# New due times and a new transfer model in the list scheduler of a spectral filter with a gated feed-forward

## The chip, the cores and the metric

The kernel runs on one core of one Trainium2 chip. The metric is the device time of one execution in microseconds (us). Before the change three timed runs gave 418.05, 418.27 and 419.44 us, the median is 418.27.

The engines are called as in the profile: PE (TensorE, matrix products), PEld (its weight load), DVE (VectorE), ACT (ScalarE), POOL (GpSimd) and SP (SyncE, which issues the DMA transfers). SPq is SP's queue.

## The reference

The input x has 2048 rows of 512 values. Cut to what matters:

```python
xn = _layernorm(x, axis=-1)
X = jnp.fft.rfft2(xn, axes=(-2, -1)) * (w_r + 1j * w_i)
s = jnp.fft.irfft2(X, s=(2048, 512), axes=(-2, -1))
gate = xn @ W_gate                      # 512 x 1376
up = xn @ W_up
h = gate * (gate > 0) * up
return x + s * silu(h @ W_down)         # 1376 x 512
```

So there are two branches from the same normalised rows: a global filter in the frequency domain over both axes, and a feed-forward with a rectified gate. Their product is added to x.

## The kernel before, in words

**Precision.** All matrix products run in f16, with each factor split into a high and a low half. Three passes (high by high, high by low, low by high) are summed in PSUM. The halves are made by ACT (high) and DVE (low), so each factor passes through both. Scales that are powers of two keep the halves in range; they are worked out on the chip from the weights themselves.

**The feed-forward** goes over four row blocks c = 0 to 3 of 512 rows and eleven tiles f of the 1376 hidden columns. `gu{c}_{f}_0` is the gate product and `gu{c}_{f}_1` the up product, each of 12 matmuls of 128x512; they have two accumulators in all. ACT makes `r`, DVE `h32 = r * up` and the low half in `h16`. `dn{c}_{i}` is the down product, for four quarters i of the output (dn0_23 holds quarters 2 and 3), with weights `wds` against `h16`. The weights come in seven groups g (`raw{g}`, loaded in f32; `wgu{g}` after the split; group 6 holds the tiles 9 and 10, `wgt` the last). For each group a small product `sum{g}` adds sums of squares over the partitions, and `p{g}` becomes its scale.

**The scale of the down weights** needs all groups: DVE reduces `md` to one column, the transfer `row_md` writes it to DRAM as a row (128 values), `rows_md` reads it back broadcast to all partitions, DVE takes `max_md` and makes `scd`. Only then can the eleven `wds` tiles be split, high half by ACT, low half by DVE, and the first dn follow (`greatest`, `down_scale` and `down_weights`, from L602, L620 and L642). The filter has the same pair of transfers, `row_mw` and `rows_mw`, after ACT has squared the eight loads `rw0` to `rw7` (`filter_scale`, L652).

**The filter** works on eight chunks. For each 256 rows, DVE folds the normalised rows (`eo`, `ee`, `xs`), they are split to `xs16`, `s1_{c}` is the first transform on PE, and its split result `t1_{c}` goes to DRAM (`A_d`, four transfers of 256 KB for two chunks). When all chunks are there, `at_{q}` reads A_d back for eight chunks q of frequencies, across all rows. Each goes through the PE products `y`, `xx`, `z` and `v`, with the filter `wt_{q}` on DVE and POOL between xx and z. The results go to DRAM (`C_d`), come back as `ct_{c}`, and `s2_{c}` is the last transform (`last_stage`); DVE unfolds it (`ye`, `sv`), multiplies by the gate and adds x (`xt`), and `out` is written.

**The transposed rows** that the feed-forward needs, `xT{c}`, come from x16 by a DMA transpose on SP's queue, one for each 256 rows (`turn`, from L406), except those of block 0, which PE turns.

**What sets the order.** Nothing is issued when it is written. Each operation is recorded as a step with an engine, an estimated cost, what it reads and writes, and perhaps a due time (`step`, L109). `run` (L128) then passes due times back along the dependencies, and builds a schedule by list: among the steps that can begin soon on an engine it takes the one with the earliest due time. It keeps a model of the free time of each engine, of one shared DMA path and of the buffers of each pool (`k4` with 12 buffers holds x16, xs and xs16 among others). The steps are issued in the order of the modelled start times, one in-order stream per engine, and an engine that meets a wait holds all that stands behind it. As all steps are issued there, nearly all instructions have line L73 in the profile.

The due times come from the tables at L33 to L50: `FIRSTS` for the first stage of the eight chunks, `MIDS` for the chunks of frequencies, `LASTS` for the last stage, `DOWN` and `FILTER` for the two scales, `STAGES`, `LOADS` and `LEADS` for normalising and loading.

Of the kernel before, what the change touches and what calls it, by code (L numbers as in the profile page):

```python
# [15 lines left out]
S, D, F = 2048, 512, 1376  # L16
# [13 lines left out]

T0, DOWN, FILTER, TICK = -0.157, 96.244, 153.189, 1.169  # L33
FIRSTS = [58.53, 65.2, 93.07, 106.1, 121.7, 135.1, 152.7, 170.3]
MIDS = [159.33, 168.39, 174.23, 204.59, 230.67, 248.77, 265.67, 291.5]
STAGES = [10.61, 2.71, 12.71, 21.79]
LASTS = [290.55, 307.89, 309.81, 329.49, 347.94, 358.12, 368.92, 380.6]
ENDS = [6.8, 11.54]
LOADS, LOADX = [4.73, 0, 8.57, None, None, None, None], [-30, -0.3]
FOLDS, FOLD_LEAD, MARGIN = ['DVE', 'DVE', 'DVE', 'DVE', 'DVE', 'DVE', 'DVE', 'DVE'], 33.902, 1.95  # L40
# [4 lines left out]
SQUARES, HALF = 32.321, 2  # L45
# [3 lines left out]
HALVES, HEADS, STATS = ('gu', 'F'), [None, 8.91], ((0, 1),)  # L49
LEADS = [None, 7.77, 8.01, 11.9, 7.52, 7.23, 8.44]  # L50


RANGES = ((0, 257, 0), (257, 512, 1))
# [26 lines left out]
class Plan:  # L80
# [25 lines left out]
        if name:  # L106
            self.tile(name, tag, None)

    def step(self, engine, cost, fn, reads=(), writes=(), due=None, lead=None, port=False, kb=0, margin=0., lag=None, mode=0):  # L109
# [3 lines left out]
        s.mode = mode  # L113
# [12 lines left out]
        return s  # L126

    def run(self):  # L128
        steps = self.steps
        for s in reversed(steps):  # L130
            s.due = 1e9 if s.due is None else s.due
            for d in s.deps:
                t = s.due - d.cost - d.lag
# [19 lines left out]
        for _ in steps:  # L153
            best = None
            for e, mine in todo.items():
                at = []
                for s in mine:
                    t = max([free[e]] + [d.end + (0. if d.engine == e == "PE" else d.lag + s.margin) for d in s.deps])
                    if s.lead is not None:
                        t = max(t, s.due - s.lead)  # L160
                    if s.port:
                        t = max(t, ports["POOL" if e == "DVE" else "DVE"])
# [6 lines left out]
                    for tag, k in need.items():  # L169
                        t = max(t, sorted(room[tag])[k - 1] + .15)  # L170
                    at.append((t, s))
                if at:
# [4 lines left out]
                    t, s = min(now, key=lambda k: (e == "PE" and k[1].mode != mode if mode else 0, k[1].due, k[1].order))  # L177
# [7 lines left out]
            t, s = best  # L185
# [9 lines left out]
            free[e] = t + s.cost  # L195
            s.end = free[e]
            if s.kb:
                dma = max(dma, s.end) + s.kb / 340
                s.end = dma
            if s.port:  # L200
                ports[e] = s.end
            for n in holds[s]:
# [40 lines left out]
def kernel(ctx: ExitStack, tc: tile.TileContext, x, wg, wu, wd, wl, ew, sp, c_r, c_d, c_m, c_x, c_s, out):  # L243
# [162 lines left out]
    def turn(c, lows):  # L406
# [12 lines left out]
        def run():  # L419
            xt = T[f"xT{c // 2}"][:, 2 * (c % 2):2 * (c % 2) + 2]  # L420
            SP.dma_start_transpose(xt.rearrange("p i k r -> p (i k) r"), x16().rearrange("p i h d -> p (i h d)"))
        step("SP", 3.4, run, reads=[(f"x16_{c}", i, h) for i in range(2) for h in range(2)], 
             writes=[(f"xT{c // 2}", j, h) for j in range(2 * (c % 2), 2 * (c % 2) + 2) for h in range(2)], kb=100)

    def keep_busy(n):

# [824 lines left out]
```

## Time and profile before

| | before |
|---|---|
| median of 3 runs | 418.27 us (418.05 to 419.44) |
| profiled execution | 418.02 us |
| its span | 416.2 us |
| mean granted TensorE clock | 0.992 of full speed |
| PE busy | 401.3 us, 96% of the span |
| DVE busy | 305.0 us, 73% |
| ACT busy | 190.4 us, 46% |
| DMA | 51.79 MB, 124 GB/s over the span |

The span reaches from the first to the last instruction of the profiled execution. A row of the timelines has the start and the length of a run of like instructions in us, engine, line, operation, output<-input by the program's names without buffer numbers, the count, and in brackets the idle time ahead of it and what ended that. A row on waits has the engine that waited, what it waited for, the sum in us, how often, and the longest. A row on windows has a stretch, its length, and for each engine busy time and instructions, then the granted clock. A row on transfers has the count, the size and the us from issue to landing.

### The profile page before, as it was taken

What the parts mean: (1) busy time and instruction counts of PE and PEld (TensorE: products, weight loads), DVE (VectorE), ACT (ScalarE), POOL (GpSimd) and SP (SyncE); (2) the same over time, 40 slices, a digit from 0 to 9 for tenths busy, and PEclk for the clock granted to TensorE, in tenths of its full rate; (3) what the DMA queues carried; (4) which work ended last, traced back from release to release, by engine and by line L of the source; (5) the groups of instructions that cost most, each with busy time, mean ns of one, the idle gap of its engine ahead of it and who ended that gap; (6) DMA issues with size and microseconds to landing.
All of it is one profiled execution on the core that took longest, in us unless ns stands there. A gap on an engine that the chain in (4) does not pass through costs nothing.

```text
span 416.2 us, 7641 instructions
## 1 busy us (share of the span) xinstructions
PE 401.3 (96%) x3004; PEld 213.0 (51%) x3004; DVE 305.0 (73%) x656; ACT 190.4 (46%) x368; POOL 47.8 (11%) x72
## 2 busy tenths in 40 slices
PE   8999999899999998949999999999999999999996
PEld 6954445344444444416555555555554445444545
DVE  4889993998899969413998538768684326978984
ACT  5989833653454657113236334344434227224311
POOL 0000000000000000000631003303130007105400
PEclk9999999999999999988999999999999999999999
DMA  7970002218242996891000860035222184683342
GB/s 259 407 264 0 0 2 107 59 44 203 77 126 56 295 332 112 111 253 63 1 2 0 267 228 2 2 92 168 73 52 51 52 194 110 202 250 105 103 153 101
DMA packets 36436, 51.79 MB, mean 124 GB/s; under 512 B 15856, under 2 KB 17744, under 8 KB 36400
## 3 DMA queue, kind: packets, MB, share of 16 engines
q1 hardware_dynamic: 36400, 51.31, 42.2%
q8 instruction: 23, 0.38, 0.4%
q14 instruction: 13, 0.11, 0.1%
HBM read 35.55 MB, written 12.60 MB: 116 GB/s over the span
## 4 chain that ended last, share of the span: by engine, by line
PE 75%; DVE 12%; DMA 8%; ACT 2%; SPq 2%; issue 1%; DVEq 0%
PE gu L73 40%; PE dn L73 21%; PE z L73 3%; PE xx L73 3%; DVE h L73 2%; PE s L73 2%; DMA row_md<-md 2%; DVE wgu L73 2%; PE y L73 2%; DMA xT<-x 2%; DVE wds L73 2%; PE small L73 2%; DVE xs L73 2%; SPq L73 2%; PE v L73 2%; DMA at<-A_d 1%
## 5 line engine op out<-in xcount | busy, mean ns | idle before, releaser
L73 PE MATMUL gu<-xT,wgu 128*128 128x512 f16 (+1 forms) x960 | 208.3, 374 | 2.7 <-DVE h L73 2.2
L73 PEld LDWEIGHTS <-wgu 128*128 128x128 f16 x960 | 92.9, 98 | 109.6 <-issue 5.9
L73 PE MATMUL dn<-wds,h 128*128 128x512 f16 (+2 forms) x528 | 117.2, 372 | 1.9 <-DVE wds L73 1.5
L73 PEld LDWEIGHTS <-h 128*128 128x128 f16 (+1 forms) x594 | 54.4, 98 | 59.8 <-issue 5.4
L73 DVE TENSOR_TENSOR h<-gu,r 128x512 f32<-128x512 f32 (+3 forms) x52 | 33.1, 636 | 29.5 <-PE gu L73 28.0
L73 ACT ACTIVATE r<-gu 128x512 f32<-128x512 f32 (+2 forms) x44 | 25.7, 584 | 47.2 <-PE gu L73 47.1
L73 POOL TENSOR_TENSOR po<-tt,tt 128x256 f32<-128x256 f32 x16 | 14.6, 915 | 281.9 <-DVE tt L73 235.4
L73 ACT ACTIVATE h<-h 128x512 f16<-128x512 f32 (+1 forms) x44 | 27.3, 624 | 40.8 <-DVE h L73 40.6
L73 DVE TENSOR_TENSOR h<-h,h 128x512 f16<-128x512 f32 (+1 forms) x44 | 30.1, 692 | 7.3 <-ACT h L73 7.1
L73 POOL TENSOR_TENSOR ae<-zz 128x128 f32<-128x128 f32 (+1 forms) x32 | 20.1, 661 | 62.8 <-ACT zz L73 62.7
L73 DVE SCALAR_TENSOR_TENSOR tt<-xsp,cw,wt 128x512 f32<-128x512 f32 x32 | 26.1, 878 | 0.0
L73 ACT ACTIVATE g<-dn,cdi 128x512 f32<-128x512 f32 (+1 forms) x16 | 10.6, 672 | 29.9 <-PE dn L73 29.9
L73 DVE TENSOR_TENSOR z<-z,z 128x1024 f16<-128x1024 f32 x8 | 9.7, 1221 | 10.6 <-ACT z L73 10.6
L73 PE MATMUL gu<-xT,wgt 128*64 128x256 f16 (+1 forms) x144 | 17.0, 309 | 0.0
L73 ACT ACTIVATE a<-y 128x1024 f16<-128x1024 f32 x8 | 8.1, 1022 | 17.6 <-PE y L73 17.5
L73 DVE TENSOR_TENSOR a<-y,a 128x1024 f16<-128x1024 f32 x8 | 9.8, 1221 | 7.4 <-ACT a L73 7.4
L73 DVE TENSOR_TENSOR sv<-sv,g 128x512 f32<-128x512 f32 (+2 forms) x18 | 11.3, 661 | 4.8 <-ACT g L73 4.6
L73 DVE SCALAR_TENSOR_TENSOR wgu<-raw,p,wgu 128x512 f16<-128x512 f32 x20 | 14.2, 746 | 0.6 <-ACT wgu L73 0.6
L73 ACT ACTIVATE xs<-xs 128x1024 f16<-128x1024 f32 x8 | 8.3, 1053 | 13.1 <-DVE xs L73 13.1
L73 ACT ACTIVATE t<-v 128x1024 f16<-128x1024 f32 x8 | 8.1, 1022 | 13.1 <-PE v L73 13.1
L73 DVE TENSOR_TENSOR t<-v,t 128x1024 f16<-128x1024 f32 x8 | 9.7, 1222 | 5.9 <-ACT t L73 5.9
L73 PE MATMUL y<-cm,at 64*128 64x64 f16 x384 | 8.3, 201 | 5.8 <-DMA at<-A_d 5.8
(151 smaller groups left out, 455.1 us busy)
## 6 DMA issues: line engine op xcount, KB each, us to landing
A_d<-t SPq DMA_DIRECT2D x16, 256.0 KB, 3.9
rw<-in_wl SPq DMA_DIRECT2D x8, 512.0 KB, 6.5
wt<-in_wl SPq DMA_DIRECT2D x8, 512.0 KB, 4.8
at<-A_d SPq DMA_DIRECT2D x8, 512.0 KB, 6.6
C_d<-t SPq DMA_DIRECT2D x16, 256.0 KB, 3.5
ct<-C_d SPq DMA_DIRECT2D x16, 256.0 KB, 5.1
xt<-in_x SPq DMA_DIRECT2D x16, 256.0 KB, 4.1
out<-xt SPq DMA_DIRECT2D x15, 256.0 KB, 2.0
```

Of the source, the lines that this page charges most:

```text
L73: return lambda *args, **kw: self.tc.keep_in_program_order(f(*args, **kw))
```

## The change

The scheduler's model gets three new numbers, and every table of due times gets new values. The model now says of a DMA transpose that it costs SP 2.0 us instead of 3.4, that it moves 1300 KB on the DMA path instead of 100 (`TURNKB`), and that it blocks SP until 2.0 us after the DMA path is free (`block`). Other transfers go at 320 instead of 340 KB per us from 40 us on (`RATE`), and land 0.6 us later (`SLACK`). No step is added or removed, and no step's instructions change.

```diff
-T0, DOWN, FILTER, TICK = -0.157, 96.244, 153.189, 1.169
-FIRSTS = [58.53, 65.2, 93.07, 106.1, 121.7, 135.1, 152.7, 170.3]
...
+T0, DOWN, FILTER, TICK = 1.2, 93.937, 134.179, 1.169
+FIRSTS = [53.32, 98.69, 53.46, 108.61, 118.2, 143.13, 197.12, 178.58]
...
+RATE, SLACK, TURNKB = 320, .6, 1300
...
             if s.kb:
-                dma = max(dma, s.end) + s.kb / 340
-                s.end = dma
+                if s.block:
+                    s.end = free[e] = max(s.end, dma + s.block)
+                dma = max(dma, s.end) + s.kb / (340 if t < 40 else RATE)
+                s.end = dma + (SLACK if t > 40 else 0.)
...
-        step("SP", 3.4, run, reads=[(f"x16_{c}", i, h) for i in range(2) for h in range(2)], 
-             writes=[(f"xT{c // 2}", j, h) for j in range(2 * (c % 2), 2 * (c % 2) + 2) for h in range(2)], kb=100)
+        step("SP", 2., run, reads=[(f"x16_{c}", i, h) for i in range(2) for h in range(2)], 
+             writes=[(f"xT{c // 2}", j, h) for j in range(2 * (c % 2), 2 * (c % 2) + 2) for h in range(2)], kb=TURNKB, block=2.)
```

What it moves is seen in the order of the instructions. The first place is SP's queue between the scale of the filter and the first read of A_d (at_0). Before:

```order
L73 DMA row_mw_111<-mw_92 128x1
L73 DMA cm1_1884<-in_c_m 128x512
L73 DMA wt_1_1914<-in_wl 128x1024
L73 DMA_TRANSPOSE xT3_1825<-x16_7_1761 128x16x128
L73 DMA A_d_69<-t1_6_1912 128x1x1024 x2
L73 DMA A_d_69<-t1_7_1923 128x1x1024 x2
L73 DMA rows_mw_112<-row_mw_111 128x128
L73 DMA cm2_1977<-in_c_m 128x512
L73 DMA wt_1_1914<-E_d_71 2x2x128
L73 DMA wt_2_2005<-in_wl 128x1024
L73 DMA at_0_2017<-A_d_69 128x2x1024
```

and now the same place of SP's queue, from row_mw to at_0:

```order
L74 DMA row_mw_111<-mw_92 128x1
L74 DMA wt_0_1707<-in_wl 128x1024
L74 DMA cm1_1774<-in_c_m 128x512
L74 DMA E_d_71<-edge2_115 64x2x16 x2
L74 DMA rows_mw_112<-row_mw_111 128x128
L74 DMA A_d_69<-t1_5_1776 128x1x1024 x2
L74 DMA wt_0_1707<-E_d_71 2x2x128
L74 DMA A_d_69<-t1_6_1865 128x1x1024 x2
L74 DMA A_d_69<-t1_7_1876 128x1x1024 x2
L74 DMA wt_1_1928<-in_wl 128x1024
L74 DMA_TRANSPOSE xT3_1932<-x16_6_1631 128x16x128
L74 DMA at_0_1973<-A_d_69 128x2x1024
```

The writes of t1_6 and t1_7 have moved from behind the transposes of x16_6 (which stood just ahead of the first piece) and x16_7 to ahead of both; rows_mw has moved ahead of the writes, and the transpose of x16_7 behind at_0.

The second place is PE around sum6, the last of the sums that the scale of the down weights needs; its weights are named in the LDWEIGHTS rows. Before:

```order
L73 LDWEIGHTS wgu4_81
L73 MATMUL gu0_6_1_661<-xT0_267,wgu4_81 128x512
L73 MATMUL sum6_689<-m6_548,ones_94 128x4
L73 LDWEIGHTS wgu5_82
L73 MATMUL gu0_7_1_691<-xT0_267,wgu5_82 128x512
```

and now, on the same engine:

```order
L74 LDWEIGHTS wgu5_82
L74 MATMUL gu0_7_1_725<-xT0_237,wgu5_82 128x512
L74 MATMUL sum6_750<-m6_609,ones_94 128x4
L74 LDWEIGHTS wgu5_82
L74 MATMUL gu0_8_0_753<-xT0_237,wgu5_82 128x512
```

sum6 has moved from ahead of the products gu0_7_0 and gu0_7_1 to behind both. The third place is DVE right behind scd, where the low halves of the down weights (wds) are made. Before:

```order
L73 TENSOR_SCALAR scd_91<-rho_86,pd_107 128x11
L73 SCALAR_TENSOR_TENSOR wds_85<-wds_85,scd_91 128x512
L73 TENSOR_TENSOR h32_0_9_839<-gu0_9_1_801,r0_9_817 128x512
L73 SCALAR_TENSOR_TENSOR wds_85<-wds_85,scd_91 128x512
L73 TENSOR_TENSOR h16_0_9_842<-h32_0_9_839,h16_0_9_842 128x512
```

and now, on DVE from scd on:

```order
L74 TENSOR_SCALAR scd_91<-rho_86,pd_107 128x11
L74 TENSOR_TENSOR t1_0_899<-s1_0_847,t1_0_899 128x2x448
L74 SCALAR_TENSOR_TENSOR wds_85<-wds_85,scd_91 128x512
L74 TENSOR_TENSOR t1_0_899<-s1_0_847,t1_0_899 128x2x64
L74 TENSOR_TENSOR t1_2_917<-s1_2_874,t1_2_917 128x2x448
L74 SCALAR_TENSOR_TENSOR wds_85<-wds_85,scd_91 128x512
```

The large piece of t1_0 has moved ahead of the first low half of wds, and those of t1_2 between the first and the second. Besides, dn0_23 of tile 0 now follows dn0_0 and dn0_1 of tile 0 on PE, where before dn0_0 and dn0_1 of ten tiles came first; s1_6 and s1_7 stand ahead of gu1_8_1; the s2 steps of chunks 4, 6, 7 and 5 stand earlier in the last row block; and on SP the loads of x2 and x3 stand ahead of the last weight group, the first rw loads ahead of those of x6 and x7.

More of the change, by code (lines that the diff above doesn't have):

```diff
@@ L28 @@
 TAIL_COLS = ((0, 0, 96, 0, 256), (1, 64, 96, 96, 352), (1, 0, 64, 128, 192))
-T0, DOWN, FILTER, TICK = -0.157, 96.244, 153.189, 1.169
-FIRSTS = [58.53, 65.2, 93.07, 106.1, 121.7, 135.1, 152.7, 170.3]
[L35 to L40, printed above, removed]
+T0, DOWN, FILTER, TICK = 1.2, 93.937, 134.179, 1.169
+FIRSTS = [53.32, 98.69, 53.46, 108.61, 118.2, 143.13, 197.12, 178.58]
+MIDS = [150.3, 160.34, 188.08, 192.0, 219.21, 237.31, 253.81, 275.45]
+STAGES = [0, 12.12, 20.71, 25.24]
+LASTS = [286.02, 290.71, 285.79, 312.67, 324.45, 353.1, 333.77, 342.56]
+ENDS = [21.7, 8.89]
+LOADS, LOADX = [-0.52, -0.11, 3.18, None, None, None, None], [-30, -0.3]
+FOLDS, FOLD_LEAD, MARGIN = ['DVE', 'DVE', 'DVE', 'DVE', 'DVE', 'DVE', 'DVE', 'DVE'], 97.974, 1.95
 HIGH_ACT = {(0, 1), (2, 1), (0, 0), (3, 1), (2, 0), (3, 0)}
@@ L44 @@
 BUSY, LATE = 42, 0.4
-SQUARES, HALF = 32.321, 2
+SQUARES, HALF = 43.857, 2
 HURRY, SLOW, SLOW_TO = -2.352, 1, 20
@@ L48 @@
 ALONE, EVAC, WHOLE = (((0,), (1,)), ((0, 1),)), ("ACT", "DVE"), .95
-HALVES, HEADS, STATS = ('gu', 'F'), [None, 8.91], ((0, 1),)
-LEADS = [None, 7.77, 8.01, 11.9, 7.52, 7.23, 8.44]
+HALVES, HEADS, STATS = ('gu', 'F'), [None, 13.67], ((0, 1),)
+RATE, SLACK, TURNKB = 320, .6, 1300
+LEADS = [None, 6.55, 6.95, 7.64, 6.43, 6.38, 7.22]
 RANGES = ((0, 257, 0), (257, 512, 1))
@@ L107, in within, with step @@
             self.tile(name, tag, None)
-    def step(self, engine, cost, fn, reads=(), writes=(), due=None, lead=None, port=False, kb=0, margin=0., lag=None, mode=0):
+    def step(self, engine, cost, fn, reads=(), writes=(), due=None, lead=None, port=False, kb=0, margin=0., lag=None, mode=0, block=0.):
         s = Step()
@@ L112, in step @@
         s.lag = self.LAG[engine] if lag is None else lag
-        s.mode = mode
+        s.mode, s.block = mode, block
         s.order, s.names, s.end, s.holder = len(self.steps), [*reads, *writes], None, self.holder
```

## The prediction

> **What bounds the kernel now.** I read the engine table first, then the list of what TensorE (PE) waited for, then the clock in the stretches around the longest wait, and last the timelines of PE, SP and VectorE (DVE) ahead of each wait.
>
> ```profile
> PE 401.3 (96%) x3004; PEld 213.0 (51%) x3004; DVE 305.0 (73%) x656; ACT 190.4 (46%) x368; POOL 47.8 (11%) x72
> PE y L73 <- DMA at<-A_d: 5.8, 1, 5.8
> PE gu L73 <- DVE h L73: 2.2, 2, 1.6
> PE dn L73 <- DVE wds L73: 1.5, 3, 0.8
> PE small L73 <- DVE md L73: 1.1, 1, 1.1
> PE gu L73 <- DVE xT L73: 0.5, 1, 0.5
> ```
>
> PE is busy 401.3 of 416.2 us. Both programs issue the same matmuls, so only PE's idle time and its clock can change. The idle time is nearly all in this list: one wait of 5.8 us, one of 1.6, some short ones. The next rows give each stretch, its length, the busy time (and instructions) of PE, PEld, DVE, ACT and POOL, PE's granted clock, DMA share and GB/s.
>
> ```profile
> 156.83:160.24 3.41, 1.78 (x9) 0.71 (x8) 3.41 (x12) 1.86 (x2) 0.00 (x0) 1.00 0.26 89
> 180.72:184.14 3.42, 1.15 (x6) 0.30 (x4) 0.57 (x3) 0.58 (x1) 0.00 (x0) 1.00 0.87 182
> 184.14:187.55 3.41, 0.00 (x0) 0.00 (x0) 0.66 (x7) 0.00 (x0) 0.00 (x0) 0.50 0.98 332
> 187.55:190.97 3.42, 3.34 (x105) 3.15 (x105) 0.25 (x2) 1.02 (x1) 0.00 (x0) 0.50 0.41 158
> 190.97:194.38 3.41, 3.41 (x60) 1.75 (x59) 2.66 (x4) 1.02 (x1) 0.00 (x0) 1.00 0.00 0
> ```
>
> The 5.8 us wait costs more than itself. The clock is half from 184.14 to 190.97, two stretches of 3.41 us, the first beginning after one in which PE was 1.15 us busy (34%). In the second PE works for 3.34 us at half speed: **1.67 us** lost. The 1.6 us wait lies in a stretch still 52% busy, and no half clock follows it.
>
> **Term 1: the wait of `y` (-5.75 and -1.67 us).**
>
> ```profile
> 159.81 1.82 SPq L73 DMA_TRANSPOSE xT<-x  x1
> 163.31 0.35 SPq L73 DMA_DIRECT2D row_mw<-mw  x1
> 165.72 9.28 SPq L73 DMA_TRANSPOSE xT<-x  x1
> 175.10 3.20 SPq L73 DMA_DIRECT2D A_d<-t  x4
> 181.69 1.54 SPq L73 DMA_DIRECT2D at<-A_d  x3
> 166.60 1.49 DVE L73 TENSOR_TENSOR t<-s,t 128x896 f16<-128x896 f32 x3 [0.51 <-ACT t L73]
> 161.88 1.51 PE L73 MATMUL s<-xs,cR 64*64 64x257 f16 x48
> 172.63 9.24 PE L73 MATMUL dn<-wds,h 128*128 128x512 f16 x42
> 187.63 0.29 PE L73 MATMUL y<-cm,at 64*128 64x64 f16 x4 [5.75 <-DMA at<-A_d]
> ```
>
> The last t (chunks 6 and 7) was ready at 168.1, but SP stood in the transpose of chunk 7 from 165.72 to 175.00. The A_d writes went out behind it, at_0 at 181.69 behind them, and it landed 5.9 us later. Now the four A_d writes stand ahead of both transposes, and s1_6, s1_7 stand 6.5 us of PE work earlier: 30 matmuls of dn and gu went from ahead of them to behind (42 matmuls of this form take 9.24 us, so one 0.216).
>
> The new times. s1_6 starts near 161.88 - 6.5 - 1.6 (the wait that goes in term 2) + 0.2 (term 3) = 154.0. In the old run t was ready 168.1 - 161.88 = 6.2 us after that start; in the new DVE order less stands between, so 158.8 to 160.2, and I take 159.5. Four writes take 3.2 us to issue and wt_1 0.4, so the transpose of chunk 6 is issued at about 163. It holds SP for 1.82 to 9.28 us (both above), so at_0 goes out between 165 and 172.5 and lands 6 to 6.6 us later:
>
> ```profile
> A_d<-t SPq DMA_DIRECT2D x16, 256.0 KB, 3.9
> at<-A_d SPq DMA_DIRECT2D x8, 512.0 KB, 6.6
> ```
>
> So at_0 lands between 171 and 179.1. PE reaches y0, which stands 1.95 us of work earlier than before: the old dn work ended at 181.87, less 1.95, less 1.63, plus 0.2 to 1.7 from term 3: 178.5 to 180. The wait is gone with about 4 us to spare at a middling transpose and with none at a 9.28 us one. With the wait goes the half clock behind it. I take **-7.4 us**; if the cover is used up, the price is the overrun, 0 to 1 us.
>
> **Term 2: the wait of `gu` on `h` (-1.63 us).**
>
> ```profile
> 147.34 6.01 SPq L73 DMA_TRANSPOSE xT<-x  x1
> 155.49 1.43 DVE L73 TENSOR_TENSOR xs<-eo 128x256 f32<-128x256 f32 x4 [4.05 <-DMA xT<-x]
> 158.46 0.68 DVE L73 TENSOR_TENSOR h<-gu,r 128x512 f32<-128x512 f32 x1
> 159.20 2.75 PE L73 MATMUL gu<-xT,wgu 128*128 128x512 f16 x12 [1.63 <-DVE h L73]
> ```
>
> xs of chunk 6 took over the buffer that the transpose of chunk 5 read; that transpose sat 6 us on SP, DVE stood for 4.05 us, and the h behind it freed PE's accumulator 1.63 us late. In the new order xs6 takes a buffer from t1_1, whose A_d write stands ahead of all rw loads on SP. The xs work still stands ahead of that h, and I work out only about 0.5 us of slack, so the new wait lies between 0 and 1.63 us. I take 0, since the 4.05 us in front of it is what made it.
>
> **Term 3: the start of the down product (+0.2 us, then a clock loss of +1.5).** Here the change moves things the wrong way.
>
> ```profile
> 51.08 0.28 PE L73 MATMUL sum<-m,ones 128*128 128x4 f32 x2
> 72.31 4.06 PE L73 MATMUL dn<-wds,h 128*128 128x512 f16 x18
> 103.80 2.75 PE L73 MATMUL gu<-xT,wgu 128*128 128x512 f16 x12
> 54.25 0.33 SPq L73 DMA_DIRECT2D row_md<-md  x1
> 63.35 0.33 SPq L73 DMA_DIRECT2D rows_md<-row_md  x1
> 68.52 0.29 DVE L73 TENSOR_REDUCE max_md<-rows_md 128x1 f32<-128x128 f32 x1 [4.59 <-DMA rows_md<-row_md]
> 69.40 0.23 DVE L73 TENSOR_SCALAR scd<-rho,pd 128x11 f32<-128x11 f32 x1
> 70.42 0.75 DVE L73 SCALAR_TENSOR_TENSOR wds<-wds,scd 128x512 f16<-128x512 f32 x1 [0.79 <-ACT wds L73]
> 71.96 0.75 DVE L73 SCALAR_TENSOR_TENSOR wds<-wds,scd 128x512 f16<-128x512 f32 x1 [0.19 <-ACT wds L73]
> 77.35 1.09 DVE L73 TENSOR_TENSOR t<-s,t 128x896 f16<-128x896 f32 x1
> ```
>
> The chain is sum6, p6 and md on DVE, row_md out (9.10 us until rows_md could go), rows_md back (5.17 us), max_md, scd, the first wds. PE reached dn at 72.31 with no wait to speak of. Now sum6 stands behind the 24 matmuls of gu0_7, 24 x 0.216 = 5.18 us later, ending at 56.5. In the old run 2.9 us passed from its end to row_md, with DVE still on other work; the new order puts p6 and md straight together (1.3 us by the seven short operations), so row_md goes out at 57.8. Then 57.8 + 9.10 + 5.17 = 72.1 for max_md, 73.2 for the end of scd. A t1_0 of 1.09 us now stands between scd and the first low wds (0.75 us): 75.1. PE arrives at 72.3 as before and **waits 2.8 us**.
>
> Behind that it gains. Before, 31.49 us passed from 72.31 to 103.80 for 132 dn matmuls (a quarter of the 528), 132 x 0.216 = 28.5 us of work: 3.0 us were lost to wds, which came one each 1.54 us at best while PE used one in 1.30 (six matmuls). Now quarters 2 and 3 (dn0_23) stand among quarters 0 and 1, so PE uses one in up to 2.6 us; adding the DVE rows between the wds I find one wait left, 0.4 us at f=9. The sum is 2.8 + 0.4 - 3.0 = **+0.2 us**. If row_md took as little as rows_md (5.17 us), the new wait would vanish and the term be -2.6; if DVE comes to p6 late by what it had in hand before (1.6 us), it is +1.8.
>
> The clock: the 2.8 us fall into one stretch of 3.41 us whole or for the larger part, or across two. The rows above show half clock after a stretch with 2.27 us idle and full clock after one with 1.63. The stretches keep their own beat: an idle part of 2.27 us or more in one comes in 1.6 of 3.41 places, one of 1.63 or more in 2.9 of 3.41. So half clock follows with a chance of 47 to 86%, and I take 62%. It costs half of one stretch, 1.7 us, less the 0.2 of the f=9 wait that it covers: **+1.5 us**.
>
> The Trainium skill, page "TensorE: Matmul & The Clock Gate", tells of a free-running window of about 3.4 us, and in "Why this matters for your kernels" it asks for no idle gap above some 3 us. This trace's 3.41 us stretches agree with the window. By the gap rule a wait of 2.8 us would leave the clock full, and the sum would be 1.5 us lower.
>
> **The rest (0, bounds 0 to +1.5).** The s2 steps of the last stage now stand at two places 18 to 19 us earlier on PE, which unloads DVE before the end. A block of sv and xt of chunks 2 and 0 (12 operations) now stands ahead of h of tile 5 in the last row block.
>
> ```profile
> L73 DVE TENSOR_TENSOR sv<-sv,g 128x512 f32<-128x512 f32 (+2 forms) x18 | 11.3, 661 | 4.8 <-ACT g L73 4.6
> ```
>
> At some 0.6 us apiece the block and the four ye pieces take 8.6 us, and that h ends about 0.7 us before PE needs its accumulator. I count nothing, and 1 us if DVE is late. The tail after PE's last matmul is unchanged.
>
> **The sum.** Against the profiled execution's 418.02 us (span 416.2, and 0.25 below the median of 418.27): 418.02 - 5.75 - 1.67 - 1.63 + 0.2 = 409.2 with full clock after the new wait, and **410.7** with half clock.
>
> **The rivals.**
>
> *Full clock at dn (409.2 us).* The 2.8 us split across two stretches, or fall under the threshold between 1.63 and 2.27 us. This is the page's gap rule as a mechanism of this kernel, and the rest of the sum stands. Chance 0.26, against 0.44 for my forecast.
>
> *The wait of `y` is only moved.* at_0 stands behind one transpose still. If that holds SP for over 9.3 us, or t comes 2 us late, PE waits 1 to 4 us at y0: 411.5 to 414.7. For it: the 9.28 us row, in which the transpose stood behind loads in flight, and now the A_d writes and wt_1 are in flight there. Against it: 1.82 and 6.01 us in the other two rows. Chance 0.15.
>
> *Slower: SP stands in front of rows_mw.* rows_mw reads what row_mw wrote, and now stands ahead of the A_d writes of chunks 5, 6 and 7, where before it stood behind them. SP would wait there until row_mw landed.
>
> ```profile
> 163.13 0.15 DVE L73 TENSOR_REDUCE mw<-mw 128x1 f32<-128x10 f32 x1
> row_mw<-mw SPq DMA_DIRECT2D x1, 0.5 KB, 8.0
> ```
>
> row_mw took 8.0 us. In the new DVE order mw stands 3 us ahead of h of tile 6, about 141; then SP is free at 150, before t is ready at 159.5, and nothing is lost. From row_mw at 151.5 on each us late moves the A_d writes, and after some 4 us of slack PE. With a middling transpose and the half clocks of both waits (412.4 us by then), PE would have to wait 7 us more at y0 to be over 419.3: row_mw at 162.5, about as late as in the old run (163.31). It needs the squares of the rw loads on ACT to come as late as before, though these loads now stand earlier on SP. Chance 0.07, at 419 to 423.
>
> *The change does nothing where it matters* (waits stay, 417 to 419): 0.04. The orders of SP, DVE and PE do differ at all three places, so I give it little. The last 0.04 is for faster than 408, above all by a shorter row_md.
>
> **How the numbers follow.** The likeliest case gives 410.7 us. The range runs from 408.3 (full clock and 0.9 gained at a shorter md chain) to 414.7 (the moved wait at its worst); it leaves out about 0.15. A measurement here tells about 0.3%, 1.25 us, from no change. Faster: 0.44 + 0.26 + 0.15 + 0.04 = 0.89; same 0.04; slower 0.07.
>
> **What would show it.** Right: in the list of PE's waits, at<-A_d is gone or below 1 us, gu<-h has no 1.6 us, and dn<-wds has one of 2.5 to 3.2 us near 72 to 75; A_d of chunks 6 and 7 is issued before 163; the granted clock is full near 185 and half for 3.4 us after 75. Wrong: row_mw issued after 151 with SP waiting behind it; a transpose above 9 us ahead of at_0; a new wait of PE on DVE in the last row block; or no wait at dn, if md comes sooner than 57.8.

## The result and the profile after

The changed kernel takes 407.12 us (median of 5 runs, 406.17 to 407.30), the kernel before 418.05 (417.48 to 419.44) beside it: a ratio of 0.973, with a 95% interval of 0.9708 to 0.9752. The gain of 10.9 us is larger than the 7.3 to 7.6 us forecast, and the time lies below the range of 408.3 to 414.7 us. The profiled execution took 406.56 us, 11.46 us less than the one before; its span is 404.8 us, against 416.2.

Read first, as before, the engine table and the list of what PE waited for, now of the changed kernel:

```profile
PE 398.4 (98%) x3004; PEld 211.2 (52%) x3004; DVE 305.0 (75%) x656; ACT 190.8 (47%) x368; POOL 50.4 (12%) x72
PE small L74 <- DVE md L74: 1.1, 1, 1.1
PE gu L74 <- DVE h L74: 0.6, 1, 0.6
PE gu L74 <- DVE xT L74: 0.5, 1, 0.5
PE dn L74 <- DVE wds L74: 0.5, 1, 0.5
```

The 5.8 us wait of y on at is gone, and so is the 1.6 us one of gu on h (the 0.6 us that is left stands at the start, as before). At dn only 0.5 us is left, where a wait of 2.8 us was forecast. The next rows are PE's timeline at the start of dn, and what leads to it on SP and DVE:

```profile
55.49 0.28 PE L74 MATMUL sum<-m,ones 128*128 128x4 f32 x2
71.70 0.38 PE L74 MATMUL dn<-wds,h 128*128 128x512 f16 x1
72.60 28.49 PE L74 MATMUL dn<-wds,h 128*128 128x512 f16 x131 [0.52 <-DVE wds L74]
100.92 5.35 PE L74 MATMUL gu<-xT,wgu 128*128 128x512 f16 x24
57.29 0.33 SPq L74 DMA_DIRECT2D row_md<-md  x1
65.01 0.33 SPq L74 DMA_DIRECT2D rows_md<-row_md  x1
69.77 0.29 DVE L74 TENSOR_REDUCE max_md<-rows_md 128x1 f32<-128x128 f32 x1 [1.62 <-DMA rows_md<-row_md]
71.80 0.74 DVE L74 SCALAR_TENSOR_TENSOR wds<-wds,scd 128x512 f16<-128x512 f32 x1
```

The last row shows the first low half of wds ready at 72.54, against 75.1 forecast. All other 131 matmuls of dn then run in 28.49 us with no wait, and the clock stays full. The stage takes 29.22 us (71.70 to 100.92) against 31.49 before.

Around the former y wait the changed kernel's SP and PE read:

```profile
142.00 0.33 SPq L74 DMA_DIRECT2D row_mw<-mw  x1
150.39 0.33 SPq L74 DMA_DIRECT2D rows_mw<-row_mw  x1
155.98 3.15 SPq L74 DMA_DIRECT2D A_d<-t  x4
160.20 4.37 SPq L74 DMA_TRANSPOSE xT<-x  x1
164.76 0.94 SPq L74 DMA_DIRECT2D at<-A_d  x2
175.43 0.23 PE L74 MATMUL y<-cm,at 64*128 64x64 f16 x4
```

```profile
184.00:188.00 4.00, 4.00 (x25) 2.15 (x23) 3.56 (x7) 1.28 (x3) 1.10 (x1) 1.00 0.03 6
```

A_d goes out at 156 and not 175, at_0 at 165 and not 182, and y begins without a wait; the window row shows the full clock (1.00) where it was half. row_mw, issued at 163.31 before, is now issued at 142.00: the due time of the filter's scale, `FILTER`, fell from 153.189 to 134.179. The experiments show that for the y wait this row matters most.

### The profile page after: what moved, and what is told of

Its sections match the earlier page's. It is cut to its first block, busy times and chain, and to the rows that moved or that the text cites. A ratio compares the mean times of both kernels' runs of the same rounds, so it can differ in the third digit from the quotient of the medians.

```text
span 404.8 us, 7658 instructions
## 1 busy us (share of the span) xinstructions
PE 398.4 (98%) x3004; PEld 211.2 (52%) x3004; DVE 305.0 (75%) x656; ACT 190.8 (47%) x368; POOL 50.4 (12%) x72
## 4 chain that ended last, share of the span: by engine, by line
PE 89%; DMA 5%; DVE 4%; ACT 1%; issue 0%; POOL 0%; DVEq 0%
PE gu L74 49%; PE dn L74 28%; PE z L74 3%; PE xx L74 3%; PE s L74 3%; DMA row_md<-md 2%; DMA x<-in_x 2%; PE y L74 2%; PE v L74 2%; DMA rows_md<-row_md 1%; PE dn_3bb L74 0%; PE dn_3b L74 0%; ACT wgu L74 0%; DVE eo L74 0%; ACT xT L74 0%; DVE xT L74 0%
## 5 line engine op out<-in xcount | busy, mean ns | idle before, releaser
L74 PE MATMUL dn<-wds,h 128*128 128x512 f16 (+2 forms) x528 | 116.0, 373 | 0.5 <-DVE wds L74 0.5
L74 POOL TENSOR_TENSOR ae<-zz 128x128 f32<-128x128 f32 (+1 forms) x32 | 21.2, 696 | 49.9 <-ACT zz L74 39.6
L74 POOL TENSOR_TENSOR pf<-tt,tt 128x256 f32<-128x256 f32 x16 | 14.8, 941 | 4.9 <-issue 3.6
L74 ACT ACTIVATE z<-z 128x1024 f16<-128x1024 f32 x8 | 8.2, 1021 | 13.3 <-PE z L74 13.3
L74 DVE TENSOR_TENSOR p<-pf,p 128x1024 f16<-128x1024 f32 x8 | 9.8, 1225 | 5.6 <-ACT p L74 5.6
```

The costliest lines, as they stand in the source:

```text
L74: return lambda *args, **kw: self.tc.keep_in_program_order(f(*args, **kw))
```

## The experiments

The kernels below, but for the two on max_md and the two unaltered ones, are the kernel before or the changed one with steps moved in the finished order, just ahead of issuing it. The frame is the same in all of these, and only the body of `moved` is shown further on (`at` gives the places of an engine's steps that read or write a name):

```diff
         order.sort(key=lambda k: k[0])
-        self.log = order
+        self.log = order = self.moved(order)
         for t, s in order:
             s.fn()
+
+    def at(self, order, engine, *names):
+        return [n for n, (t, s) in enumerate(order) if s.engine == engine and all(k in s.names for k in names)]
```

### The transpose of chunk 7 moved in the kernel before

```diff
+turn, = self.at(order, "SP", ("xT3", 3, 0))
+read, = self.at(order, "SP", "at_1")
+order.insert(read, order.pop(turn))
```

> The kernel before, with one step moved on SP: the transpose of chunk 7 stands behind at_1 instead of ahead of the A_d writes of chunks 6 and 7. Theory (the y wait comes from that transpose alone): t is ready at 168.1 as before, the A_d writes go out there, rows_mw still waits for row_mw until about 171.5, at_0 is issued near 174 and lands near 180, before PE comes to y0 at 181.9. The wait of 5.75 us and the half clock behind it go: about 418.0 - 7.4 = 410.6 us. Rival (the writes were late for another reason, rows_mw above all, or loads in flight): the wait falls by less than 3 us, the clock stays half behind it, 414 us or more.

416.44 us (413.97 to 417.54), a ratio of 0.9947 (0.9923 to 0.9971): 2 us, not 7.4. PE's wait list of this run:

```profile
PE y L73 <- DMA at<-A_d: 3.3, 1, 3.3
PE gu L73 <- DVE h L73: 2.4, 2, 1.9
```

More than half of the y wait stayed, and the half clock with it. That SP merely stood in the transpose, as the prediction explained term 1, is at most a part of the cause.

### The transpose of chunk 5 as well

```diff
+late = [n for name in ("cD", "rw6") for n in self.at(order, "SP", name)]
+turn, = self.at(order, "SP", ("xT2", 3, 0))
+steps = [order[n] for n in [turn, *late]]
+order = [k for n, k in enumerate(order) if n not in [turn, *late]]
+load, = self.at(order, "SP", "rw7")
+order[load:load] = steps
```

> As the run before it, and besides the transpose of chunk 5 stands three loads earlier on SP (ahead of cD, rw6 and rw7). Theory (the 1.63 us wait of gu on h comes from that transpose through a buffer of DVE): DVE's 4.05 us wait on it falls below 2 us, the gu wait goes, and the time is 1.6 us below the run with the one transpose moved, about 409.0 us. What is left to the changed kernel (407.1) is then the down product's stage and the start. Rival (the h is late for the DVE work ahead of it): the gu wait stays above 1 us and the time is the same as with the one move.

411.56 us (410.70 to 413.51). The gu wait of 1.9 us is gone, so its cause, the transpose of chunk 5, is shown. But the y wait was still there:

```profile
PE y L73 <- DMA at<-A_d: 2.7, 2, 1.7
PE gu L73 <- DVE h L73: 0.6, 1, 0.6
```

The fall was 4.9 us and not 1.6: all that hangs on h came earlier too, t among it (A_d was issued at 164.4, not 168.3), and the y wait shrank to where the clock held.

### The order on SP undone in the changed kernel

```diff
+late = [n for c in (6, 7) for n in self.at(order, "SP", ("t1_%d" % c, 1, 1))] + self.at(order, "SP", "at_0") + self.at(order, "SP", "at_1")
+steps = [order[n] for n in late]
+order = [k for n, k in enumerate(order) if n not in late]
+turn, = self.at(order, "SP", ("xT3", 3, 0))
+order[turn + 1:turn + 1] = steps
```

> The changed kernel with one part undone: on SP both transposes (chunks 6 and 7) stand ahead of the A_d writes of chunks 6 and 7 and of at_0 and at_1 again. Theory: the first transpose is issued at about 160, the two hold SP 9 to 14 us, the writes go out at 169 to 174 and at_0 lands at 181 to 186, while PE comes to y0 at 175: a wait of 6 to 11 us and 1.7 us of half clock, 414 to 420 us. Rival (PE order carries it: s1_6 and s1_7 stand early enough that the SP order is free): a wait below 3 us, under 411 us.

407.15 us (406.27 to 407.95): the same as the changed kernel. With both transposes ahead of the writes again, SP reads:

```profile
158.28 5.45 SPq L74 DMA_TRANSPOSE xT<-x  x2
163.78 3.73 SPq L74 DMA_DIRECT2D A_d<-t  x4
170.37 0.91 SPq L74 DMA_DIRECT2D at<-A_d  x2
```

Both transposes together hold SP for 5.45 us, where the one of chunk 7 alone held it 9.28 before. So the order that the first place of the change shows is not needed, at least with s1 as early as it now stands, and the transpose of chunk 7 is not slow by itself. Something in the kernel before made it slow.

### dn0_23 apart again in the changed kernel

```diff
+late = self.at(order, "PE", "dn0_23")[:10]
+steps = [order[n] for n in late]
+order = [k for n, k in enumerate(order) if n not in late]
+last = self.at(order, "PE", "dn0_0", ("wdl", 9))[0]
+order[last + 1:last + 1] = steps
```

> The changed kernel with one part undone on PE: dn0_23 of the tiles 0 to 9 stands behind dn0_0 and dn0_1 of tile 9 again instead of among them. Theory (the interleaving closes the loss in the down product's stage): PE uses a tile of weights in 1.30 us while DVE makes one each 1.87 us in its new order, so by tile 9 PE has waited about 9 x 0.57 = 5 us or a little more, in pieces below 1 us that leave the clock full: 411.5 to 414 us. Rival (the shorter wait for row_md is what closed it): the time stays within 1.5 us of the changed kernel.

412.59 us (412.28 to 412.79), 5.5 us more. The wait list and one of its ten waits, on PE's timeline:

```profile
PE dn L74 <- DVE wds L74: 4.1, 10, 1.0
87.84 1.46 PE L74 MATMUL dn<-wds,h 128*128 128x512 f16 x6 [0.42 <-DVE wds L74]
```

Six matmuls (1.30 us and the pipe's end) and a wait, ten times over: without the interleaving the changed kernel's slower flow of wds would cost more than it did before. The interleaving is what closes the stage, as the prediction had it.

### The wait at dn made as long as forecast, and longer

`max_md` is taken ten times (nine in vain) in the first, nineteen times in the second kernel:

```diff
-        step("DVE", .22, lambda: DVE.tensor_reduce(top, rows, axis=AX.X, op=ALU.max), reads=[f"rows_{name}"], writes=[f"all_{name}"], due=due + 10)
+        def tops():
+            for _ in range(10 if name == "md" else 1):
+                DVE.tensor_reduce(top, rows, axis=AX.X, op=ALU.max)
+        step("DVE", .22, tops, reads=[f"rows_{name}"], writes=[f"all_{name}"], due=due + 10)
```

> The changed kernel with the maximum max_md taken ten times instead of once (the same result nine times more), which delays scd and the first wds by about 2.3 us, so that PE waits at the first dn about as long as was predicted for the change, 2.8 us. Theory A (a stretch of 3.41 us with some 2.3 us or more idle is followed by half clock; in about half to four fifths of the runs): profile with half clock for 3.4 us behind the wait, time +2.3 and in most runs +1.5 more, 409 to 411 us. Theory B (only a gap above some 3 us does it): clock full in all runs, +2.3 us, about 409.4.

411.92 us (411.36 to 412.61). The start of dn in this run on PE's timeline, and the window behind it (after the busy times the granted clock):

```profile
74.85 0.38 PE L74 MATMUL dn<-wds,h 128*128 128x512 f16 x1 [2.92 <-ACT wds L74]
75.75 30.13 PE L74 MATMUL dn<-wds,h 128*128 128x512 f16 x131 [0.52 <-DVE wds L74]
```

```profile
74.00:78.00 4.00, 2.62 (x7) 0.95 (x7) 4.00 (x8) 2.33 (x4) 0.00 (x0) 0.73 0.19 41
```

A wait of 2.9 us is followed by half clock: the 131 matmuls take 30.13 us against 28.49, 1.64 us more, and 2.9 + 1.64 is 4.5 of the 4.8 us that the runs are longer. Each of its four runs is longer by at least 4.2 us than the changed kernel's median, so the half clock came each time. So a wait close to the forecast 2.8 us did bring about the clock loss that the prediction put at 1.5 us.

> The same with nineteen times: the wait at the first dn grows by about 4.8 us to some 5.3 us. Both theories of the clock expect half clock for 3.4 us or more behind it: +4.8 + 1.5 = 413.4 us. If the time is only 4.8 us longer, half clock behind a wait costs nothing here, since the weights wds bind then.

414.92 us (414.15 to 415.86), 7.8 us more. The wait was 5.95 us, and 131 matmuls took 31.10 us: 2.6 us of half clock.

### Both kernels unaltered, for a second profile

> The changed kernel unaltered, for a second profile. Theory (row_md's time from issue to landing varies from run to run between 7.7 and 9.1 us): it differs from 7.7 us by some tenths or more, and the wait at the first dn with it. Rival (it depends on the program): 7.7 us within 0.2.

> The kernel before unaltered, for a second profile. Theory (row_md varies from run to run): not 9.1 us again. Rival (it depends on the program): 9.1 us within 0.2. The first 48 us of PE show whether the 0.7 to 1.1 us that the changed kernel was ahead by there belong to the change or to where the clock's stretches fall.

407.61 and 420.13 us (one execution each). From row_md to rows_md passed 7.92 us in the first and 9.30 in the second:

```profile
57.80 0.33 SPq L74 DMA_DIRECT2D row_md<-md  x1
65.72 0.33 SPq L74 DMA_DIRECT2D rows_md<-row_md  x1
```

```profile
54.06 0.33 SPq L73 DMA_DIRECT2D row_md<-md  x1
63.36 0.33 SPq L73 DMA_DIRECT2D rows_md<-row_md  x1
```

So the difference belongs to the program: over all runs, 9.1 to 9.8 us in the eight of the kernel before and its variants, 7.1 to 7.9 us in the nine of the changed kernel with row_md at 57 to 58. The 0.6 us by which PE was ahead at 72 us in the first profile of the changed kernel does not: in this second one it came to dn at 72.2 us, as before the change.

### at_0 and at_1 right behind the A_d writes, in the kernel before

```diff
+turn, = self.at(order, "SP", ("xT3", 3, 0))
+read, = self.at(order, "SP", "at_1")
+order.insert(read, order.pop(turn))
+reads = self.at(order, "SP", "at_0") + self.at(order, "SP", "at_1")
+steps = [order[n] for n in reads]
+order = [k for n, k in enumerate(order) if n not in reads]
+write = self.at(order, "SP", ("t1_7", 1, 1), ("A_d", 7, 1))[0]
+order[write + 1:write + 1] = steps
```

> The kernel before, with SP's order changed at one place: the four A_d writes of chunks 6 and 7, then at_0 and at_1, all ahead of rows_mw, cm2, the piece of E_d for wt_1, wt_2 and the transpose of chunk 7. t is ready at 168 as before. Theory (with only the transpose moved, the y wait fell to 3.3 us, since at_0 still stood behind transfers that SP had to wait for: rows_mw, the piece for wt_1 until 175.2, wt_2): A_d out from 168.2, landed near 174.5, at_0 issued there and landed near 179.5, before PE comes to y0 at 182: no wait, full clock, 6.5 to 7.5 us below the kernel before. Rival (t itself is too late: from t to landed A_d and back takes over 13.8 us whatever stands between): a wait of 2 us or more stays.

417.73 us (416.51 to 418.51), a ratio of 0.9981 (0.9967 to 0.9996). The SP rows, and the lines of the transfers in the window from 158 to 180 us, which give the busy share of the DMA engines in tenths and the GB/s in 40 equal slices of 0.55 us:

```profile
162.86 0.35 SPq L73 DMA_DIRECT2D row_mw<-mw  x1
167.51 2.97 SPq L73 DMA_DIRECT2D A_d<-t  x4
178.17 0.90 SPq L73 DMA_DIRECT2D at<-A_d  x2
```

```profile
DMA  0000299992259099189795563643059999950055
GB/s 0 0 0 0 57 216 214 217 207 46 31 13 114 0 89 34 4 84 43 41 35 20 37 22 15 37 30 30 7 231 406 402 399 402 391 212 0 0 67 160
```

Here the cause begins to show. A_d is out at 170.5, but SP waits until 178.17 for it to land. In the 20 slices from the tenth to the one before 231 GB/s, 163 to 174 us, with transfers waiting, all 16 engines together move 0 to 114 GB/s, though three of these slices, with 34, 43 and 35 GB/s, show them 90% busy or more; then 400. The slow stretch begins where row_mw, 128 writes of 4 bytes, goes out. The transpose's 9.28 us in the kernel before lay in such a stretch too. From this came the theory for the runs further down, that everything behind row_mw crawls.

The time of this run does not tell against an early at_0, though. Its waits of PE on y, and the row of DVE that explains the longer one:

```profile
PE y L73 <- DVE am L73: 4.3, 1, 4.3
PE y L73 <- DMA at<-A_d: 0.4, 1, 0.4
185.22 0.29 DVE L73 TENSOR_REDUCE max_mw<-rows_mw 128x1 f32<-128x128 f32 x1 [9.91 <-DMA rows_mw<-row_mw]
```

In spite of the crawl at_0 came almost in time: y0 waited 0.4 us. But rows_mw, now behind at_1, went out only at 179.12, DVE stood 9.91 us in front of max_mw, and am, a copy of a part of at that stands behind it on DVE and that the y products need, held PE for 4.3 us. In the kernel before DVE stood there too, for 7.74 us, but that did not decide: am had to wait 2.80 us more for at_0. No run moves at_0 forward and the scale back on DVE while row_mw stays.

### s1 of the chunks 6 and 7 put back in the changed kernel

```diff
+def moves(s):
+    n = set(s.names)
+    return n & {"s1_6", "s1_7"} or s.engine == "SP" and n & {("t1_6", 1, 1), ("t1_7", 1, 1), ("xT3", 1, 0), "wt_1", "at_0", "at_1", ("xT3", 3, 0)} and ("E_d", 0) not in n
+late = [k for k in order if moves(k[1])]
+rest = [k for k in order if not moves(k[1])]
+order = sorted(rest + [(t + 6.5, s) for t, s in late], key=lambda k: k[0])
```

> The changed kernel with s1_6 and s1_7 put back behind gu1_9_0 on PE (6.5 us later, as before), and all that hangs on them (t1, the A_d writes, the transposes of chunks 6 and 7, at_0 and at_1, in the order of the changed kernel) behind. Theory (the earlier s1 is what made the y wait go, with either order on SP): t is ready at 162.6, at_0 lands some 13.5 us later, as in the changed kernel, at 176, when PE comes to y0 at 175.5 to 176.5: the slack of about 6 us is used up, and a wait of 0 to 2 us shows; 407 to 409 us, or 411 with half clock. Rival (the order on SP alone was enough, with much to spare): no wait and the same time.

408.08 us (406.48 to 408.55). The profile has no y wait; A_d went out at 161.95, at_0 at 170.47, and DVE had at_0 at 175.18, as y began (175.14). The slack of the earlier s1 is all used up, yet at most 1 us is lost (the runs of the two kernels overlap): that move, too, was hardly needed. With it and the order on SP both undone there is no run.

### sum6 earlier in the changed kernel

```diff
+late = self.at(order, "PE", "sum6")[:1]
+chain = [n for n in self.at(order, "DVE", "p6") + self.at(order, "DVE", "mdt") if not any(k[0] == "wgu" for k in order[n][1].names if isinstance(k, tuple))]
+chain = sorted(set(chain))[:3]
+one, steps = [order[n] for n in late], [order[n] for n in chain]
+order = [k for n, k in enumerate(order) if n not in late + chain]
+fold = self.at(order, "DVE", ("eo2", 1))[0]
+order[fold:fold] = steps
+gu, = self.at(order, "PE", ("gu0_7_1", 0, 1))
+order[gu:gu] = one
```

> The changed kernel with sum6 put one product earlier on PE (ahead of gu0_7_1) and p6 and md ahead of the fold of chunk 2 on DVE, so that row_md is issued near 54.3, as in the kernel before. Theory (row_md takes 9.1 to 9.8 us when a 16 KB instruction load of about 3 us falls behind its issue, as in all four runs of the kernel before and its variants, and 7.5 to 7.9 us when that load comes first, as in the six of the changed kernel): row_md takes over 9 us, so rows_md is issued at 63.5 to 64, only 1.2 us earlier and not 3; the wait of 0.5 to 1.0 us at the first dn goes: 406.1 to 406.6 us. Rival (the length belongs to the program's other order, x2 and x3 loaded ahead): row_md takes 7.5 to 7.9 us and rows_md goes out at 62.

406.48 us (405.64 to 406.67). row_md went out at 55.61 and took 7.76 us, so the theory in its first form fell; PE did not wait at dn. The ratio to the kernel before, 0.9706 (0.9681 to 0.9731), can't be told from the changed kernel's 0.973.

> The changed kernel with sum6 two products earlier on PE (ahead of gu0_7_0) and p6 and md on DVE ahead of the second low half of wgu5, so that row_md goes out near 53.5 to 54.5, some 2 us ahead of the 16 KB instruction load at 56.3, as in the kernel before. Theory (an instruction load that falls into the crawl behind row_md makes it land 1.5 to 2 us later; in the run with row_md at 55.61 the load came 0.7 us behind it and did not): row_md takes 9.1 to 9.8 us and the load about 3 us. Rival (the length belongs to something else in the kernel before): 7.5 to 7.9 us. Either way no wait at the first dn: 406 to 407 us.

(The same, with `("wgu", 8, 0, 1), ("wgu", 8, 1, 1)` for the place on DVE and `("gu0_7_0", 0, 0)` on PE.) 406.64 us (406.10 to 406.67). row_md at 54.23 took 8.11 us, between the two groups; the 16 KB instruction load came 2.3 us behind it and took 3.6 us, where such loads take about 1 us elsewhere. So the load does run slowly there, as in the kernel before (2.8 to 3.3 us), but that it alone makes the 1.5 to 2 us isn't shown.

### row_mw moved away from the transpose in the kernel before

```diff
+scale = sorted(set(self.at(order, "DVE", "all_mw")))
+steps = [order[n] for n in scale]
+order = [k for n, k in enumerate(order) if n not in scale]
+first = min(n for n, (t, s) in enumerate(order) if "cw" in s.names)
+order[first:first] = steps
+row = self.at(order, "SP", "row_mw")
+steps = [order[n] for n in row]
+order = [k for n, k in enumerate(order) if n not in row]
+read, = self.at(order, "SP", "at_1")
+order[read + 1:read + 1] = steps
```

> The kernel before, with row_mw and rows_mw moved on SP from their place ahead of the transpose of chunk 7 to behind at_1, and the scale that hangs on them moved on DVE to just ahead of its first reader; the transposes, the A_d writes, s1 and all else stand as before. Theory (while row_mw's 128 writes of 4 bytes are under way, some 8 us, everything behind them on the DMA queue crawls; the 9.28 us hold of the transpose and the late A_d writes are that, not the transpose itself): the transpose of chunk 7 holds SP 4 to 6 us instead of 9.3 to 10.1, A_d goes out at 170 to 171, at_0 is issued near 176 and lands near 181, about when PE comes to y0 (181.9): the y wait falls from 5.8 or 6.6 us below 1.5 us, and the half clock goes with it: 410.5 to 412 us. Rival (the DMA path is full with transposes and loads anyway): the transpose holds SP for over 8 us again, and the time stays within 2 us of the kernel before.

418.46 us (416.72 to 419.63): the time did not move. But the profile shows both halves of the theory. SP and PE of this run:

```profile
165.99 3.13 SPq L73 DMA_TRANSPOSE xT<-x  x1
169.22 3.21 SPq L73 DMA_DIRECT2D A_d<-t  x4
175.70 0.90 SPq L73 DMA_DIRECT2D at<-A_d  x2
160.03 4.44 PE L73 MATMUL gu<-xT,wgu 128*128 128x512 f16 x12 [2.31 <-DVE h L73]
192.06 1.46 PE L73 MATMUL y<-cm,at 64*128 64x64 f16 x48 [2.98 <-DMA at<-A_d]
```

At its old place, the transpose now holds SP for 3.13 us, and y0 does not wait. What was gained there was lost again at y2: its at_2 stands behind rows_mw, in front of which SP waited 9.0 us for row_mw to land, and the clock is half behind the y2 wait (0.50 from 192 to 196 us). In the profiled execution there is a half clock behind a gu wait of 2.31 us as well (12 matmuls in 4.44 us, not 2.75).

With row_mw and rows_mw behind at_2 (the `"at_1"` of the diff becomes `"at_2"`):

> As the run in which row_mw stood behind at_1 (there the transpose of chunk 7 held SP for 3.1 us instead of 9.3, the wait at y0 was gone, and a wait of 3.0 us came up at y2, whose at_2 stood behind row_mw), but with row_mw and rows_mw behind at_2 as well. Theory (row_mw ahead of the transpose was the whole cause of the y wait): no y wait above 1 us, 410 to 412.5 us (what stays is the 1.6 to 2.3 us wait of gu on h, with half clock behind it in some runs, and the loss at dn). Rival (the waits only move on): the time stays above 415 us.

411.41 us (410.89 to 411.81), 0.9832 (0.9808 to 0.9857): 6.9 us from one small transfer moved, with its read-back and the scale that hangs on it. Its wait list has no y wait of note, and the GB/s of the window from 160 to 190 us (slices of 0.75 us) show no long gap while transfers wait (one slice at 31), where the kernel before has one from slice 6 to slice 18. Before:

```profile
GB/s 0 127 212 218 145 23 68 25 82 5 12 90 46 31 16 27 33 27 326 257 289 274 171 178 309 298 240 223 73 97 193 381 240 330 328 366 412 396 197 16
```

and with row_mw behind at_2:

```profile
GB/s 6 213 214 208 142 208 273 283 195 31 205 289 174 180 270 350 208 302 148 175 311 254 232 232 227 336 396 347 164 85 33 0 0 0 0 0 0 2 20 43
```

```profile
PE gu L73 <- DVE h L73: 2.2, 2, 1.6
PE dn L73 <- DVE wds L73: 1.5, 3, 0.8
PE y L73 <- issue: 0.4, 1, 0.4
```

With the transpose of chunk 5 moved as well (the diff of the second experiment added):

> The same, and the transpose of chunk 5 ahead of cD, rw6 and rw7. Theory (two causes, both on SP: row_mw for y, the transpose of chunk 5 for the gu wait): neither wait is left, full clock, 408.5 to 409.5 us; the rest to the changed kernel (407.1) is the loss at dn, about 2 us. Rival: over 411 us.

409.70 us (409.22 to 409.85), 0.9788 (0.9766 to 0.9811). The gu wait is gone, and of the list above dn is left, and 0.3 us at y.

The changed kernel has the crawl too. This is its GB/s from 138 to 160 us (slices of 0.55 us), with row_mw issued at 142.00, and a load of 512 KB (wt_0) and one of 128 KB (cm1) right behind it:

```profile
GB/s 57 220 246 410 253 15 30 0 1 45 97 37 0 30 0 89 45 37 37 37 22 15 22 30 60 60 355 216 65 24 323 399 279 4 30 197 201 238 197 194
```

From 142 to 152 us it moves 0 to 97 GB/s, but there it holds up nothing that PE waits for: the four A_d writes go out at 155.98.

### row_mw put back in the way in the changed kernel

> The changed kernel with s1_6 and s1_7 6.5 us later, as in an earlier run that showed no y wait at all, and besides row_mw right ahead of the A_d writes of chunks 6 and 7 and rows_mw behind at_1 (the scale on DVE just ahead of its first reader). Theory (row_mw makes what stands behind it crawl): A_d is issued at 162 but lands 8 to 10 us later, the transpose of chunk 6 holds SP for over 7 us, at_0 lands at 179 to 182, PE waits 3 to 6 us at y0 with half clock behind it: 411.5 to 415 us. Rival (late s1 and SP's order alone decide, and there is slack left): no wait above 1 us, 407 to 409 us.

407.06 us (406.82 to 407.56). This does not test the theory: A_d itself waited for t until 162.57, and SP issued row_mw, which stood ahead of it, at 152.26 already, so that it had landed (after 7.8 us) by then. But it is the control for the next run, from which it differs only in the place of row_mw. There row_mw stood between wt_1 and the transpose of chunk 6 (s1 late and the scale moved on DVE, as in the diffs above):

```diff
+row, back = self.at(order, "SP", "row_mw")
+steps = [order[row], order[back]]
+order = [k for n, k in enumerate(order) if n not in (row, back)]
+read, = self.at(order, "SP", "at_1")
+order.insert(read + 1, steps[1])
+turn, = self.at(order, "SP", ("xT3", 1, 0))
+order.insert(turn, steps[0])
```

> The changed kernel with s1_6 and s1_7 6.5 us later (no y wait in that run alone) and row_mw between the load of wt_1 and the transpose of chunk 6, behind the A_d writes (in the last try it stood ahead of them and was long done). Theory: row_mw goes out at 165.6, the transpose behind it holds SP for 8 us or more instead of 4.5, at_0 goes out at 174 or later and lands at 179 to 181, PE waits 3 to 6 us at y0 with half clock behind: 411.5 to 415 us. Rival (a transpose held behind row_mw belongs to the kernel before alone): no wait above 1 us, 407 to 409 us.

413.18 us (411.37 to 415.04), 6.1 us more than the control. The wait of y is back, and the half clock (0.61 in the window):

```profile
166.11 0.87 SPq L74 DMA_DIRECT2D row_mw<-mw  x1
167.02 3.78 SPq L74 DMA_TRANSPOSE xT<-x  x1
170.98 0.96 SPq L74 DMA_DIRECT2D at<-A_d  x2
178.82 0.29 PE L74 MATMUL y<-cm,at 64*128 64x64 f16 x4 [3.31 <-DMA at<-A_d]
```

```profile
178.00:182.00 4.00, 3.18 (x104) 3.03 (x105) 0.20 (x1) 0.89 (x1) 0.00 (x0) 0.61 1.08 266
```

The price came as expected, by another row: the transpose held SP for only 3.78 us, and it was at_0, issued at 170.98, that took 7.8 us to land instead of 4.2 in the changed kernel. What is held up depends on what stands in the queue when the slow stretch begins.

## Why the prediction was wrong

**Term 1 (y, -5.75 and -1.67): the size was right, the cause wrong, so the size was luck.** y0 no longer waits and the clock there is full. But the prediction laid the 9.28 us to the transpose and to the order on SP. Undoing that order cost nothing, and putting s1 back at most 1 us (408.1); in the kernel before, moving the transpose brought little (416.4), an at_0 moved forward as well only shifted the wait to DVE (417.7), and moving row_mw, with its read-back and the scale, brought 6.9 us. In the changed kernel with late s1, row_mw put back in the way cost 5 to 6 us. So row_mw, issued at 142.00, some 14 us ahead of the writes, and not at 163.31, is enough to take the wait away. Whether the early s1 would have covered a late row_mw is open, as no run has both. The prediction quoted both rows, 163.31 for row_mw and 165.72 for the transpose, and read them as unrelated. It even priced a late row_mw in its slower rival, as a wait of SP in front of rows_mw; SP did pass rows_mw at 150.4, as forecast.

**Term 2 (gu on h, -1.63): right, and for the reason given.** The pair of runs with and without the transpose of chunk 5 moved shows it twice (4.9 us in the first, where the y wait shrank with it, 1.7 us in the second).

**Term 3 (dn, +0.2 and +1.5) is the step that failed.** It forecast that PE "waits 2.8 us" at dn; it waited 0.52 (1.03 in the second profile, where PE came 0.5 us later), and the stage was 2.27 us shorter than before instead of 0.2 longer. The chain went like this: sum6 ended at 55.8 and not 56.5 (PE was that much ahead from the start, and so came to dn earlier too), row_md was issued at 57.29 against 57.8, took 7.72 us against 9.10, rows_md 4.76 against 5.17, and max_md to the first low half 2.77 against 3.0. Most of it is row_md: its duration was taken from the one row of the kernel before, and that row belongs to that program. The sum even gave the outcome for a shorter row_md, -2.6 (at 5.17 us, which it never came near), where -2.27 was measured, but with a chance of 0.04. Why row_md is shorter in the changed program stays open. A wait as long as the prediction had it cost somewhat more than it said: with 2.92 us at dn the time was 411.92 us, against the 410.7 forecast.

**The half clock (+1.5) did not come, since the wait didn't.** The rule behind it held: half clock followed idle times of 2.31, 2.92, 3.31 and 5.95 us, and none followed 1.63 or 1.94. The Trainium skill (page "TensorE: Matmul & The Clock Gate", section "Why this matters for your kernels") asks for no idle gap above about 3 us; here gaps of 2.31 and 2.92 us were followed by half clock too, and the measurement decides.

**The sum.** By the profiles: 418.02 - 5.75 - 1.67 - 1.63 - 2.27 - 0.6 (the start, which varies from run to run) = 406.1, measured 406.56. The 4.1 us between 410.7 and 406.56 are 2.5 from dn, 1.5 from the clock and 0.6 from the start, less 0.5 of small losses. By single moves in the kernel before: 418.3 to 411.4 (row_mw), to 409.7 (transpose of chunk 5), and the remaining 2.6 us to 407.1 fit the 2.27 us of dn.

**The rest (0) and the slower rival** came out as forecast: no wait in the last row block, and rows_mw passed before t was ready.

## What to carry to other kernels

Look at what is in flight when a transfer is slow, in GB/s and not in busy share: in one run here the DMA engines were 90% busy or more in slices that moved 34 to 43 GB/s, behind half a kilobyte. Put a scatter of tiny writes where no transfer that matters stands behind it. A duration taken from one profile belongs to that program's neighbours; where a forecast hangs on one, give the shorter case a fair chance.

## What the runs showed of the hardware

- Behind a transfer of 128 writes of 4 bytes (row_mw), the DMA engines moved 5 to 90 GB/s for about 10 us in the kernel before and 0 to 97 in the changed one, where the same window without it shows mostly 140 to 350. The transpose of chunk 7 held SP for 9.3 to 10.1 us there and for 2.9 to 3.1 us without it, but one right behind row_mw in the changed kernel only for 3.8 us; writes of A_d (4 x 256 KB) landed after 8.6 us and not 3.8. That the 4 byte size is the reason was not tried.
- Such a transfer (row_md) took 7.1 to 9.8 us even with the queue nearly empty: its 144 packets are done within about 1 us (about 9 ns each), and nothing more is seen until it lands. Why it takes 9.1 to 9.8 us in one program and 7.1 to 7.9 in the other stays open; a 16 KB instruction load that began 2.2 to 2.4 us behind it ran three times as long (2.8 to 3.6 us against about 1), but one that began 0.7 us behind it took 1.3 us. The Trainium skill (page "DMA: Bandwidth & Descriptors", section "Specifications") says that the engine reads, changes and writes back what is below 512 bytes; no run here shows whether that is what takes the time.
- Half clock for 3.4 us followed a wait of PE of 2.3 us already (12 matmuls in 4.44 us instead of 2.75).
